# Grouped-query attention: fewer chunks of x transposed on TensorE, eight heads per chunk, and one weight load issued by ScalarE

## Chip, cores, metric

One core of one Trainium2 chip. The metric is device time in microseconds (us) of one execution.

Words used below. PE is TensorE, PEld its weight loads, DVE VectorE, ACT ScalarE, SP SyncE; SPq is the stretch in which SP is occupied with issuing a DMA. A **chunk** is one of the eight 128-column slices of x that the projection sums over. **Rows of chunk n** are the 128 rows of the weight matrix that belong to it. In the profile lines w_sb holds the weights of the first eight heads and wq_sb those of heads 8 and up. A DMA has **landed** when the last of its 16 semaphore increments has arrived; I read each increment as the share of one of the core's 16 DMA engines, though the trace does not name the engine.

## The reference

Two independent problems A and B, joined along the last axis:

```python
q = (x @ wq).reshape(B, Sq, Hq, Dh)      # B=16, Sq=32, D=1024, Hq=32, Dh=128
scores = einsum(q, k) * Dh**-0.5         # k, v shared by groups of 8 heads, Sk=512
o = einsum(softmax(scores), v)
out = o.reshape(B, Sq, Hq*Dh) @ wo       # bf16 throughout
```

## The kernel before

Everything after the first 20 us is a tightly interleaved stream of matmuls. The change touches only the start: the projection of problem A's first eight heads (the **first-head block**), for which x must be transposed (contraction on partitions) and the first weights fetched. SP issues nearly all loads, in program order:

```python
# NF = 6, HC = 4, DC = 8, TT = 4, REP = 8 ; load_w0(d0, d1, h0, h1): rows of chunks d0..d1, heads h0..h1
nc.scalar.preload_act_table_set("natural_log_exp_and_others")
load_x(0, 0, TT // 2)          # chunks 0,1 of x, first half of the tokens, plain, 128 KB
load_x(0, TT // 2, TT)         # second half, 128 KB
load_w0(0, 1, 0, NF // 2)      # 96 KB
load_w0(0, 1, NF // 2, NF)     # 96 KB
load_w0(1, 2, 0, NF)           # 192 KB
load_x(2, 0, TT)               # chunks 2,3 of x, plain, 256 KB
load_w0(2, 3, 0, NF)           # 192 KB
load_w0(3, 4, 0, NF)
load_w0(0, HC, NF, REP)        # heads 6,7 of chunks 0..3
load_w0(HC, HC + 1, 0, REP)    # 256 KB
load_x_transposed(HC)          # chunks 4,5 by a transposing load
load_w0(HC + 1, DC - 1, 0, REP)
load_x_transposed(HC + 2)      # chunks 6,7
load_w0(DC - 1, DC, 0, REP)
load_wq(0, 2, 0, 2)            # heads 8.. ; then keys, values, further weights
# ... cut
warm_up(22)                    # 22 matmuls on constants
# ... 8 transposes of chunks 0,1, copied out of PSUM by DVE and ACT; chunk 0 for heads 0..5
first_heads(range(0, NF - 2), (1,))
transpose_x(2, 0, TT, nc.vector.tensor_copy)     # 4 PE transposes and a PSUM copy
transpose_x(3, 0, TT, nc.scalar.copy)
first_heads(range(NF - 2, NF), (1,))
first_heads(range(NF), (2, 3))
first_q += [psum.tile(...) for _ in range(2)]    # cut
first_heads(range(NF, REP), range(HC))           # heads 6,7, chunks 0..3
first_heads(range(REP), range(HC, DC - 1))
# ... chunk 7, copies to qT, then the stream (heads 8 and up, scores, values)
```

## Time and profile before

Median 343.27 us (343.26 to 343.75, 3 runs). The page gives the busy times and the chain of work that ended last:

```profile
span 341.4 us, 5454 instructions
PE 335.0 (98%) x2082; PEld 213.2 (62%) x2121; DVE 265.6 (78%) x336; ACT 185.8 (54%) x209; POOL 46.7 (14%) x206
PE 94%; DVE 1%; issue 1%; DMA 1%; SPq 1%; ACT 0%; POOL 0%; ACTq 0%
```

PE is never free for long, and the chain runs through it. A matmul's busy time is a modelled, pipelined duration, so for exact sums I use start-to-start distances: 0.216 us for a 512-column matmul. The Trainium skill ("Trainium Kernel Development and Optimization", Performance Expectations) warns that matmul busy time says little about the distance to the limit; here it agrees, since a 512-column matmul is shown as 0.38 us long though one starts every 0.216 us. The change can therefore only matter where PE has gaps or by taking work from PE. The timeline of PE in the first 23 us (start, length, engine, line, operation, count; in brackets the idle time before it and who ended it):

```profile
0.93 2.52 PE L516 MATMUL q_ps<-const-bfloat16-1.0 128*128 128x128 bf16 x22 [0.93 <-PEq L694]
3.24 1.06 PE L524 MATMUL xT_ps<-ident,x_sb 128*128 128x128 bf16 x8
4.10 1.60 PE L534 MATMUL q_ps<-xT,w_sb 128*128 128x256 bf16 x9
6.07 1.04 PE L534 MATMUL q_ps<-xT,w_sb 128*128 128x512 bf16 x4 [0.37 <-DMA w_sb<-in_A_wq_dram]
6.94 0.61 PE L524 MATMUL xT_ps<-ident,x_sb 128*128 128x128 bf16 x8
7.61 11.62 PE L534 MATMUL q_ps<-xT,w_sb 128*128 128x512 bf16 x52
19.07 3.62 PE L301 MATMUL q_ps<-xT,wq_sb 128*128 128x512 bf16 x16
```

The block ends at 19.07, where the matmuls on wq_sb begin. It has one wait, 0.37 us for the rows of chunk 1 (landed 6.02). The second set of eight transposes costs 0.45 us in the chain.

### The profile page before, as it was taken

How to read it: one execution, taken by the hardware profiler on the slowest of the kernel's cores; microseconds unless marked ns; L12 is line 12 of the kernel's file. 1: busy time of each engine (PE TensorE's matmuls, PEld its weight loads, DVE VectorE, ACT ScalarE, POOL GpSimd, SP SyncE). 2: the span in 40 equal slices, each digit the busy share in tenths (PEclk: the TensorE clock that was granted, in tenths of full speed). 3: DMA queues.
4: the chain of work that ended last, by engine and by line, in shares of the span. 5: the costliest groups of instructions: out<-in, count | busy, mean ns of one | idle time of the engine just before them, and what ended most of it. 6: DMA issues, size and time to landing. Idle time of an engine off the chain costs nothing.

```text
span 341.4 us, 5454 instructions
## 1 busy us (share of the span) xinstructions
PE 335.0 (98%) x2082; PEld 213.2 (62%) x2121; DVE 265.6 (78%) x336; ACT 185.8 (54%) x209; POOL 46.7 (14%) x206
## 2 busy tenths in 40 slices
PE   8999999999999999999999999999999999999996
PEld 6455666666666666666666666666666666666555
DVE  1046988888988898888888988879888888889540
ACT  3058666666667667666645545555555555555110
POOL 0001110011111111110012221222122101111100
PEclk9999999999999999999999999999999999999999
DMA  6989999999999988999999956999449996340001
GB/s 192 289 166 286 287 219 241 192 198 276 302 282 203 232 231 221 212 302 288 325 274 266 276 135 142 335 256 250 117 109 292 355 206 160 95 113 10 18 18 33
DMA packets 128094, 71.70 MB, mean 210 GB/s; under 512 B 75840, under 2 KB 127296, under 8 KB 128064
## 3 DMA queue, kind: packets, MB, share of 16 engines
q1 hardware_dynamic: 127536, 70.21, 85.3%
q0 software_dynamic: 384, 1.05, 0.8%
q8 instruction: 17, 0.28, 0.3%
q14 instruction: 13, 0.11, 0.1%
q10 hardware_dynamic: 144, 0.07, 0.1%
HBM read 50.86 MB, written 2.10 MB: 155 GB/s over the span
## 4 chain that ended last, share of the span: by engine, by line
PE 94%; DVE 1%; issue 1%; DMA 1%; SPq 1%; ACT 0%; POOL 0%; ACTq 0%
PE f_ps L320 30%; PE q_ps L301 28%; PE ob L425 17%; PE s_ps L357 16%; PE q_ps L534 4%; DMA w_sb<-in_A_wq_dram 1%; DVE parts L376 1%; ACT p_sb L365 0%; SPq L465 0%; SPq L477 0%; DVE r L411 0%; DVE oT L447 0%; PE xT_ps L524 0%; DVE cs L384 0%; ACT o_sb L329 0%
## 5 line engine op out<-in xcount | busy, mean ns | idle before, releaser
L365 ACT ACTIVATE p_sb<-s_ps,shift 128x1024 bf16<-128x1024 f32 x128 | 142.6, 1114 | 97.7 <-PE s_ps L357 86.2
L376 DVE TRANSPOSE_TENSOR_REDUCE parts<-p_sb 128x32 f32<-128x1024 bf16 x128 | 158.7, 1240 | 21.0 <-ACT p_sb L365 19.3
L320 PE MATMUL f_ps<-wo_sb,oT 128*128 128x512 bf16 (+1 forms) x525 | 128.2, 366 | 0.6
L301 PE MATMUL q_ps<-xT,wq_sb 128*128 128x512 bf16 x430 | 113.3, 379 | 0.5
L425 PE MATMUL ob<-p_sb,v_sb 128*128 128x256 bf16 x512 | 76.8, 273 | 0.8
L357 PE MATMUL s_ps<-qT,kT 128*128 128x256 bf16 x512 | 76.8, 273 | 0.0
L320 PEld LDWEIGHTS <-oT 128*128 128x128 bf16 x544 | 53.2, 98 | 35.4
L357 PEld LDWEIGHTS <-kT 128*128 128x128 bf16 x512 | 56.9, 113 | 28.3
L301 PEld LDWEIGHTS <-wq_sb 128*128 128x128 bf16 x448 | 43.7, 98 | 32.4 <-DMA wq_sb<-in_A_wq_dram 0.4
L425 PEld LDWEIGHTS <-v_sb 128*128 128x128 bf16 x512 | 50.0, 98 | 20.1
L447 DVE TENSOR_TENSOR oT<-r,ob 128x512 bf16<-128x512 f32 x64 | 43.9, 686 | 19.9 <-PE ob L425 19.4
L411 DVE STREAM_TRANSPOSE r<-rall 128x512 f32<-128x512 f32 x64 | 44.2, 691 | 1.1
L309 ACT CAST qT<-q_ps 128x512 bf16<-128x512 f32 x56 | 32.6, 583 | 16.6 <-PE q_ps L301 16.6
L394 POOL COPY half<-cs 64x32 f32<-64x32 f32 x32 | 6.5, 204 | 232.0 <-DVE cs L384 232.0
L329 ACT CAST o_sb<-f_ps 128x512 bf16<-128x512 f32 (+1 forms) x17 | 9.5, 559 | 23.6 <-PE f_ps L320 23.6
L534 PE MATMUL q_ps<-xT,w_sb 128*128 128x512 bf16 (+1 forms) x65 | 14.2, 372 | 0.5 <-DMA w_sb<-in_A_wq_dram 0.4
L384 DVE TENSOR_REDUCE cs<-parts 128x32 f32<-128x128 f32 x32 | 12.1, 377 | 1.1
L406 DVE RECIPROCAL rall<-sums 128x32 f32<-128x32 f32 x32 | 10.2, 318 | 3.3 <-POOL sums L403 3.3
L534 PEld LDWEIGHTS <-w_sb 128*128 128x128 bf16 x67 | 6.4, 99 | 7.6 <-DMA w_sb<-in_A_wq_dram 0.9
L560 DVE CAST qT<-q_ps 128x512 bf16<-128x512 f32 x4 | 2.5, 684 | 10.2 <-PE q_ps L534 10.2
L331 POOL DMA_DIRECT2D out_dram<-o_sb x8 | 4.6, 574 | 29.3 <-ACT o_sb L329 29.3
L395 POOL TENSOR_TENSOR half<-half,cs 64x32 f32<-64x32 f32 x32 | 7.8, 242 | 2.6
(25 smaller groups left out, 44.8 us busy)
## 6 DMA issues: line engine op xcount, KB each, us to landing
v_sb<-in_A_v_cache_dram SPq DMA_DIRECT2D x16, 512.0 KB, 6.3
wq_sb<-in_B_wq_dram SPq DMA_DIRECT2D x8, 1024.0 KB, 5.9
wo_sb<-in_A_wo_dram SPq DMA_DIRECT2D x8, 1024.0 KB, 7.6
v_sb<-in_B_v_cache_dram SPq DMA_DIRECT2D x16, 512.0 KB, 4.6
wo_sb<-in_B_wo_dram SPq DMA_DIRECT2D x8, 1024.0 KB, 8.2
wq_sb<-in_A_wq_dram SPq DMA_DIRECT2D x5, 1024.0 KB, 6.6
wq_sb<-in_A_wq_dram SPq DMA_DIRECT2D x2, 512.0 KB, 7.4
kT<-in_A_k_cache_dram SPq DMA_TRANSPOSE x64, 4.4
```

The source lines that it names most:

```text
L301: nc.tensor.matmul(ps[:], lhsT=w[:, dc, (h % 4) * DH:(h % 4 + 1) * DH], rhs=xT[pr][:, dc, :], start=(dc == 0), stop=(dc == DC - 1),)
L309: nc.scalar.copy(out=qT[pr, g][:, :, hl, :], in_=ps[:].rearrange("p (b s) -> p b s", s=SQ),)
L320: nc.tensor.matmul(ps[:, 0:width], lhsT=oT[pr, tt][:, h, :], rhs=wo_tiles[pr, nh, h // REP][:, h % REP, off:off + width], start=(h == 0), ...
L357: nc.tensor.matmul(s_ps[:, c, :], lhsT=kT[:, i % GRP, c, :], rhs=qT[pr, g][:, b, :, :].rearrange("p h s -> p (h s)"), start=True, stop=True,)
L365: nc.scalar.activation(out=p_sb[:], in_=s_ps[:], func=ACTF.Exp, bias=shift[:], scale=SCALE)
L376: nc.vector.tensor_reduce(out=parts[k][:, q, :, :].rearrange("p c h -> p (c h)"), in_=st[i]["p"][:].rearrange("p c (h s) -> p (c h) s", s=SQ),
L384: nc.vector.tensor_reduce(out=cs[:], in_=parts.pop(k)[:].rearrange("p q c h -> p q h c"), axis=AX.X, op=ALU.add,)
L406: nc.vector.reciprocal(out=rall[:, k, :], in_=quad.pop(k)[:])
L411: nc.vector.transpose(out=r[:].rearrange("p n s -> p (n s)"), in_=rall[:, k, o * 2 * REP:(o + 1) * 2 * REP] .unsqueeze(2).to_broadcast([P, ...
L425: nc.tensor.matmul(ob[j][:, q, :], lhsT=v_sb[:, i % GRP, c, :], rhs=st[i]["p"][:, c, :], start=(c == 0), stop=(c == KC - 1),)
L447: nc.vector.tensor_tensor(out=out, in0=rcp.pop(j)[:].rearrange("p (q h) s -> p q h s", h=REP), in1=ob.pop(j)[:].rearrange("p q (h s) -> p ...
L534: nc.tensor.matmul(first_q[h][:, ts], lhsT=w0[dc // HC][:, dc % HC, h * DH:(h + 1) * DH], rhs=xT[0][:, dc, ts], start=(dc == 0 and t0 == 0 ...
```

## The change

Its intent: drop eight PE transposes and their copies by letting a transposing load bring chunks 2 and 3 of x, use each chunk for all eight heads at once with full 2 KB weight rows, and start the first weight rows sooner from ScalarE's otherwise idle queue.

```diff
+            load_w0(0, 1, 0, NF // 2, nc.scalar)
             nc.scalar.preload_act_table_set("natural_log_exp_and_others")
-            load_x(0, 0, TT // 2)
-            load_x(0, TT // 2, TT)
-            load_w0(0, 1, 0, NF // 2)
+            load_x(0, TT // 2)
+            load_x(TT // 2, TT)
             load_w0(0, 1, NF // 2, NF)
             load_w0(1, 2, 0, NF)
-            load_x(2, 0, TT)
-            load_w0(2, 3, 0, NF)
-            load_w0(3, 4, 0, NF)
-            load_w0(0, HC, NF, REP)
+            load_w0(0, 2, NF, REP)
+            load_x_transposed(2)
+            load_w0(2, 3, 0, REP)
+            load_w0(3, 4, 0, REP)
+            load_x_transposed(HC)
             load_w0(HC, HC + 1, 0, REP)
-            load_x_transposed(HC)
 ... cut (x_sb is smaller, load_w0 takes the issuing engine)
-            first_heads(range(0, NF - 2), (1,))
-            transpose_x(2, 0, TT, nc.vector.tensor_copy)
-            transpose_x(3, 0, TT, nc.scalar.copy)
-            first_heads(range(NF - 2, NF), (1,))
-            first_heads(range(NF), (2, 3))
+            first_heads(range(NF), (1,))
             first_q += [...]
-            first_heads(range(NF, REP), range(HC))
-            first_heads(range(REP), range(HC, DC - 1))
+            first_heads(range(NF, REP), (0, 1))
+            first_heads(range(REP), range(2, DC - 1))
```

More of the change, by code (lines that the diff above doesn't have):

```diff
@@ L456, in fast_path @@
             HC = DC // 2
-            x_sb = blk_tile([P, TT, HC * P], "x_sb")
+            x_sb = blk_tile([P, TT, 2 * P], "x_sb")
             xT[0] = blk_tile([P, DC, NTOK], "xT")
@@ L462, in fast_path, with load_x @@
             wq_v = A_wq.rearrange("(c p) n -> p c n", p=P)
-            def load_x(d0, t0, t1):
-                nc.sync.dma_start(
-                    out=x_sb[:, t0:t1, d0 * P:(d0 + 2) * P],
-                    in_=x_v[:, t0:t1, d0 * P:(d0 + 2) * P],
-                )
+            def load_x(t0, t1):
+                nc.sync.dma_start(out=x_sb[:, t0:t1, :], in_=x_v[:, t0:t1, 0:2 * P])
             def load_x_transposed(d0):
@@ L474, in load_x_transposed, with load_w0 @@
                 )
-            def load_w0(d0, d1, h0, h1):
-                nc.sync.dma_start(
+            def load_w0(d0, d1, h0, h1, eng=nc.sync):
+                eng.dma_start(
                     out=w0[d0 // HC][:, d0 % HC:(d1 - 1) % HC + 1, h0 * DH:h1 * DH],
```

## The prediction

> **What bounds it now.** TensorE: the page gives PE 335.0 us busy of a 341.4 us span at full granted clock, and the chain that ended last is 94% PE. The change touches only the first 20 us; I read that stretch from the timeline and the DMA issues with their landings.
>
> - PE warms up from 0.93 us, transposes x from 3.24, runs the first real matmul at 4.10; the first-head block ends near 19.1. Its 64 matmuls of 512 columns at 0.216 us are 13.8 us, so about 1.2 us of it is not matmul: the second eight transposes (0.45 us in the chain), a wait of 0.37 us for the weight rows of chunk 1 (landed 6.02), small edges.
> - After that PE is fed just in time by the SyncE queue. The tightest place is not in the block: the weights of head 12 (wq_sb issued 21.52, landed 27.27) are awaited at 27.32, with a 0.04 us bubble: slack zero. Next comes the first v_sb (landed 31.64, used 32.5).
>
> **What the change does.**
> - Removes 8 PE transposes (0.45 us) and two PSUM copies; the wait for chunk 1 should shrink, because its rows go out one issue (about 0.5 us) sooner. PE's possible gain: 0.6 to 0.9 us.
> - Replaces a plain 256 KB load of x by a transposing one. In before, one of 256 KB holds SyncE 1.33 or 2.54 us (plain: 0.43 to 0.58) and lands 5.5 to 6.0 us after issue; the first one's 256 B packets fill about 2 us of DMA (8.5 to 10.6), where 256 KB of plain 2 KB rows take about 0.8. The Trainium skill, "Advanced Engine Details and Errata", X-Bar Transpose (TRN2), says transposing DMAs "are as fast as regular DMAs"; this trace disagrees. Extra DMA time, estimated: 0.6 to 1 us. Merging weight rows to 2 KB pieces gives back 0.1 to 0.2.
> - ScalarE issues 96 KB. The skill, "DMA: Bandwidth & Descriptors", Issuing engines are not separate DMA queues, says this saves only sequencer time: here one slot of 0.5 us. Its table load (1.28 us) moves back but ends before ScalarE's first copy at 3.9. The 96 KB share the engines with x, whose second half may land 0.1 to 0.3 us later.
>
> **On the critical path.** Chunk 2 is wanted near 7.6 us. Its transposed x should land near 7.5, the weights behind it near 8.2 to 8.6: a new wait of 0.3 to 1 us, which eats the saved transposes. Chunk 4 may wait 0.2. So the block should end at 18.6 to 19.4. Then the zero-slack weights of head 12: the queue ahead of them drains 0.2 to 0.7 us later, so they land at 27.4 to 28.0. An earlier PE only waits longer there. After it PE is saturated and the shift stays to the end.
>
> **Predicted:** 343.5 us, 342.7 to 344.6. Faster by over 2%: 0.01; within 2%: 0.98; slower: 0.01. The most there is to gain (about 1 us) is 0.3%.
>
> **What would show it.** Right: 64 first-head matmuls after 8 transposes; a PE wait of 0.3 to 1 us at 7.5 to 8.6 us for transposed x or its weights; a longer wait for wq_sb before head 12; later work shifted by a constant. Wrong: no wait at chunk 2, or head 12's weights landing before 27.2.
>
> **What would make it wrong.** If early transposing loads run faster with an emptier queue, the DMA shift is zero or negative and up to 0.8 us is gained; if packets of two queues hamper each other, the first matmul slips and 1 to 2 us are lost.

## The result

344.12 us median (343.18 to 344.27, 6 runs) against 343.37 (343.26 to 343.82, 6 runs): ratio 1.0015, interval 1.0002 to 1.0028. A ratio is the mean time of one kernel's fast runs over that of the other's of the same rounds, so it is not quite the ratio of the medians. By the 2% rule this is "same"; the interval says slightly slower. One of the six runs, 343.18, was as fast as before; its trace does not exist, so why stays open.

The page after, same parts:

```profile
span 342.3 us, 5436 instructions
PE 334.5 (98%) x2074; PEld 212.6 (62%) x2113; DVE 265.1 (77%) x335; ACT 185.1 (54%) x208; POOL 46.6 (14%) x206
PE 95%; DMA 2%; SPq 1%; issue 1%; ACT 0%; ACTq 0%
```

PE has 0.5 us less work, the span is 0.9 us longer. The timeline of PE after:

```profile
0.93 2.52 PE L513 MATMUL q_ps<-const-bfloat16-1.0 128*128 128x128 bf16 x22 [0.93 <-PEq L687]
3.83 0.74 PE L521 MATMUL xT_ps<-ident,x_sb 128*128 128x128 bf16 x8 [0.38 <-DMA x_sb<-in_A_x_dram]
4.61 3.66 PE L531 MATMUL q_ps<-xT,w_sb 128*128 128x256 bf16 x19
9.61 10.53 PE L531 MATMUL q_ps<-xT,w_sb 128*128 128x512 bf16 x47 [1.35 <-DMA w_sb<-in_A_wq_dram]
19.98 3.19 PE L301 MATMUL q_ps<-xT,wq_sb 128*128 128x512 bf16 x13
```

The second set of transposes is gone; the first set waits 0.38 us for x; and a new wait of 1.35 us stands before the first matmul of chunk 2, ended by the weights, not by the transposed x. The block ends 0.91 us later. The sum, start to start: first real matmul later, +0.51 (4.10 to 4.61); the one wait for weights 1.51 instead of 0.53, +0.98; transposes, -0.45; matmuls still at half clock at the very start, -0.13 (explained at the end). That is +0.91. After the block nothing more happens: the first score matmul is 0.91 later (22.52, 23.43), the last matmul of all 0.87 (338.07, 338.94).

The chain of waits in order of time names the weight load. Before, and after:

```profile
2.73 3.29 DMA w_sb<-in_A_wq_dram
6.02 0.05 issue
6.07 1.04 PE q_ps L534 x4
```

```profile
3.21 1.33 SPq L468
4.54 0.05 issue
4.59 4.97 DMA w_sb<-in_A_wq_dram
9.56 0.05 issue
9.61 0.39 PE q_ps L531
```

After, SP is held 1.33 us by issuing the transposing load (SPq L468), then issues the rows of chunk 2 at 4.59, and these take 4.97 us to land. Before, they were issued at 3.68 and took 3.67 us. So they went out 0.91 us later and took 1.30 us longer.

A rule that these lines suggest, and that the experiments use, as long as PE's clock has risen: **the block ends at the latest of (a landing, plus the PE work that stands behind it).** Before: 6.07 plus 13.00 us of gapless PE work is 19.07. After: 9.61 plus 48 matmuls of 0.216 (10.37) is 19.98.

### The profile page after: what moved, and what is told of

Its sections match the earlier page's. It is cut to its first block, busy times and chain, and to the rows that moved or that the text cites. A ratio compares the mean times of both kernels' runs of the same rounds, so it can differ in the third digit from the quotient of the medians.

```text
span 342.3 us, 5436 instructions
## 1 busy us (share of the span) xinstructions
PE 334.5 (98%) x2074; PEld 212.6 (62%) x2113; DVE 265.1 (77%) x335; ACT 185.1 (54%) x208; POOL 46.6 (14%) x206
## 4 chain that ended last, share of the span: by engine, by line
PE 95%; DMA 2%; SPq 1%; issue 1%; ACT 0%; ACTq 0%
PE f_ps L320 31%; PE q_ps L301 28%; PE ob L425 17%; PE s_ps L357 16%; PE q_ps L531 3%; DMA w_sb<-in_A_wq_dram 1%; DMA out_dram<-o_sb 0%; SPq L468 0%; SPq L474 0%; ACT o_sb L329 0%; SPq L465 0%; ACTq L329 0%; ACT p_sb L365 0%; ACTq L365 0%
## 5 line engine op out<-in xcount | busy, mean ns | idle before, releaser
L447 DVE TENSOR_TENSOR oT<-r,ob 128x512 bf16<-128x512 f32 x64 | 43.9, 686 | 19.9 <-PE ob L425 19.4
L309 ACT CAST qT<-q_ps 128x512 bf16<-128x512 f32 x56 | 32.6, 582 | 16.6 <-PE q_ps L301 16.6
L553 ACT CAST qT<-q_ps 128x512 bf16<-128x512 f32 x4 | 2.1, 600 | 13.6 <-PE q_ps L531 13.6
```

What stands on the lines that cost most here:

```text
L309: nc.scalar.copy(out=qT[pr, g][:, :, hl, :], in_=ps[:].rearrange("p (b s) -> p b s", s=SQ),)
L447: nc.vector.tensor_tensor(out=out, in0=rcp.pop(j)[:].rearrange("p (q h) s -> p q h s", h=REP), in1=ob.pop(j)[:].rearrange("p q (h s) -> p ...
```

## The experiments

Theories at the outset. **Q** (queue order): the rows of chunk 2 land late because they stand behind the transposing load. **B/L** (bytes): what counts is how much must be in before PE can go on; by the first matmul of chunk 2 that is 1280 KB after, 1088 KB before. **A**: the ScalarE issue delays x and that is the loss. **S**: a chance late landing. Labels beginning with a_ edit the changed kernel, with b_ the kernel before. Twelve kernels were run, each with 5 rounds. The block end is that of the one profiled run, whose time lies up to 0.5 us from its kernel's median. The overview:

| label | median (before beside it) | ratio, interval | block end in trace | what set it (landing) |
|---|---|---|---|---|
| a_again | 343.87 (343.32) | 1.0014, 1.0001 to 1.0027 | 20.00 | rows of chunk 2, 9.58 |
| a_rows2_ahead | 343.89 (343.32) | 1.0017, 1.0003 to 1.0031 | 19.96 | rows of chunks 5,6, 14.72 |
| a_plain_x23 | 344.32 (343.32) | 1.0029, 1.0017 to 1.0041 | 19.93 | x chunks 2,3, 7.76 |
| a_first_on_sync | 344.37 (343.32) | 1.0029, 1.0016 to 1.0042 | 19.65 | rows of chunk 2, 9.23 |
| b_first_on_scalar | 344.06 (343.36) | 1.0019, 1.0005 to 1.0032 | 19.79 | rows of chunk 1, 6.74 |
| b_xT23 | 344.02 (343.36) | 1.0017, 1.0003 to 1.0031 | 19.88 | rows of chunk 3, 9.90 |
| b_heads8 | 345.39 (343.36) | 1.0047, 1.0033 to 1.0061 | 21.28 | rows of chunk 2, 10.00 |
| b_rows1_on_scalar | 345.88 (343.36) | 1.0067, 1.0053 to 1.0081 | 21.26 | x at 4.41, then the PE clock |
| b_rows1_scalar_late | 343.43 (343.54) | 0.9993, 0.9979 to 1.0006 | 19.23 | rows of chunk 0, heads 3 to 5, 5.54 |
| b_half1_scalar_late | 343.86 (343.54) | 1.0010, 0.9996 to 1.0023 | 19.62 | the PE clock |
| b_first_in_front | 343.35 (343.54) | 1.0004, 0.9991 to 1.0018 | 19.10 | rows of chunk 1, 6.06 |
| b_rows1_not_awaited | 343.35 (343.33) | 1.0003, 0.9989 to 1.0016 | 19.46 | the PE clock |

### a_again: the changed kernel once more

No edit.

> The changed kernel once more, for a second trace. Theory Q (queue order: the weight rows of chunk 2 stand behind the transposing load of x chunks 2 and 3 and land late because of it): the PE wait before the first chunk 2 matmul comes again at 1.0 to 1.5 us, the rows land at 9.3 to 9.8, time 344.0 to 344.3. Theory S (chance: a few of the 16 increments of that landing happened to be late, 8.65 to 9.56 against 8.06 to 8.12 for the rest): the wait differs by over 0.4 us from the first trace, and single times scatter between 343.2 and 344.3.

Measured: the rows landed at 9.58, the wait was 1.18 us in the timeline of PE, the times 343.82 to 344.26. The wait is in the expected range and within 0.2 us of the first trace, so it is no accident of one run: S falls as the explanation of the whole. The shape of the landing repeats too. In the first trace 11 of its 16 increments were in by 8.12 us and the last at 9.56; in the second 14 by 8.89 and the last two at 9.51 and 9.58. The load waits for its last one or two increments.

### a_rows2_ahead: the rows of chunk 2 ahead of the transposing load

```diff
-            load_x_transposed(2)
             load_w0(2, 3, 0, REP)
+            load_x_transposed(2)
```

> The changed kernel with the weight rows of chunk 2 issued ahead of the transposing load of x chunks 2 and 3. Theory Q: the rows land before 7.5 us, the transposed x at 7.7 to 8.3; the wait at chunk 2 falls from 1.35 to at most 0.5 us and the time to 343.2 to 343.5. Theory B (bandwidth: what counts is only how much data must be in, whatever its order): the later of the two still lands near 9.5 and the time stays at 344.0 to 344.3.

Measured: Q's landings came out: rows at 7.47 (expected before 7.5), transposed x at 8.49 (0.2 us after the expected 7.7 to 8.3), and no wait at chunk 2. Q's time did not: 343.89, the same as the changed kernel. PE's timeline shows where the wait went:

```profile
4.71 7.56 PE L531 MATMUL q_ps<-xT,w_sb 128*128 128x256 bf16 x35
12.78 7.34 PE L531 MATMUL q_ps<-xT,w_sb 128*128 128x512 bf16 x32 [0.51 <-DMA w_sb<-in_A_wq_dram]
19.96 0.81 PE L301 MATMUL q_ps<-xT,wq_sb 128*128 128x512 bf16 x3
```

The rows of chunk 4, again a load next to a transposing one, came late (13 of 16 increments by 11.23, the last at 12.74), and the rows of chunks 5 and 6 at 14.72 instead of 13.49; that landing plus its 24 matmuls is the end. So Q explains which load was late, not how much time was lost. Taking one limit away uncovered the next, 0.02 us below.

### a_plain_x23: the transposing load of chunks 2 and 3 undone

```diff
-            load_x_transposed(2)
+            load_x(2, 0, TT)
 ... and the old order of PE work, with its eight transposes
```

> The changed kernel with x chunks 2 and 3 loaded plainly again and transposed on TensorE, in the old order of TensorE work; the merged weight rows and the issue by ScalarE stay. If the transposing load is the cost (theories Q and B): no wait over 0.4 us at chunk 2, time 343.2 to 343.5, as before the change or a little under. If the issue by ScalarE is the cost (theory A: its 96 KB delay x and with it everything): time stays at 343.9 to 344.3.

Measured: 344.32, no better than the changed kernel and rather worse. There is no wait over 0.4 us at chunk 2; instead the first matmul is at 4.69, x chunks 2 and 3 land at 7.76 (6.84 before the change), and 7.80 plus 0.46 us of transposes plus 54 matmuls is the end. The time fits A, but a_first_on_sync refutes A. Note that the order of PE work is the old one here, so the early rows of heads 6 and 7 only take queue space: the run tests the transposing load, not a clean combination of the other two parts.

### a_first_on_sync: the ScalarE issue undone

```diff
-            load_w0(0, 1, 0, NF // 2, nc.scalar)
 ...
             load_x(TT // 2, TT)
+            load_w0(0, 1, 0, NF // 2)
```

> The changed kernel with the first weight rows issued by SyncE, third in its queue, as before the change. Both theories: first transposes back at 3.24 us (from 3.83), first real matmul at 4.1. Theory Q: the wait at chunk 2 then only grows by what was won plus the later issue, to 1.8 to 2.4 us, and the time is 344.1 to 344.7, no better. Theory A: about 0.5 us is won, time 343.5 to 343.8.

Measured: first transposes at 3.24, first real matmul at 4.09, as both theories said. Time 344.37, no better, as Q said. The size of the wait was missed: 0.56 us, not 1.8 to 2.4. In this trace PE ran at half clock until 6.1 us and so reached chunk 2 late by itself; and the rows landed at 9.23, a little sooner than before the edit. A alone is out: 0.5 us won at the start of the block is swallowed by the next landing. The trace is of the fastest of the five runs (343.93); why the other four took 344.25 to 344.58 is not on record.

### The three parts one at a time

**b_first_on_scalar**: only the issue by ScalarE.

```diff
+            load_w0(0, 1, 0, NF // 2, nc.scalar)
             nc.scalar.preload_act_table_set("natural_log_exp_and_others")
 ...
-            load_w0(0, 1, 0, NF // 2)
```

> The kernel before with one part of the change alone: the first weight rows issued by ScalarE. Theory A (the first x shares the DMA engines with these 96 KB): first transposes at 3.8 to 3.9 us instead of 3.24, first real matmul at 4.6 to 4.7; the rows of chunk 1 then land before they are wanted, so its wait of 0.37 us goes; first-head block ends at 19.2 to 19.4 and the time is 343.4 to 343.7. If the early slip is swallowed by a later landing all the same: 343.2 to 343.4.

Measured: 344.06; transposes at 3.90, first matmul at 4.72, as theory A said for the slip. The rows of chunk 1 did not come in time: 6.74 (6.02 before), still awaited (0.22 us), and 6.79 plus the same 13.00 us is 19.79. The loss is larger than either side expected.

**b_xT23**: only the transposing load of chunks 2 and 3.

```diff
-            load_x(2, 0, TT)
+            load_x_transposed(2)
 ...
-            transpose_x(2, 0, TT, nc.vector.tensor_copy)
-            transpose_x(3, 0, TT, nc.scalar.copy)
```

> The kernel before with another part alone: x chunks 2 and 3 by a transposing load, six heads per chunk as before. Theory Q: first matmul stays at 4.10; the rows of chunk 2, queued behind the transposing load, land at 8.8 to 9.5 and PE waits 1.2 to 2 us for them, although 0.45 us of transposes are gone; time 344.2 to 344.8. If the transposing load is harmless by itself: no wait over 0.5 us, time 342.8 to 343.2.

Measured: 344.02, a little under the expected range. First matmul 4.13. The rows of chunk 2 landed at 8.04, sooner than expected but later than with the plain load (7.34), and those of chunk 3 at 9.90 (8.14): two waits, 0.76 and 0.39 us in the timeline, for 0.45 us of transposes saved. The mechanism is Q's; the size was split over two loads. Two things differ ahead of these rows, and this run does not separate them. The transposing load held SP for 1.33 us where the plain one took 0.43, so the two loads behind it went out 0.91 and 0.98 us later. And in each half microsecond from 5.0 to 6.5 us, with the transposing load's packets under way, the DMA moved 184 to 218 GB/s at a busy share of 0.95 or more; before it was 240 to 375 GB/s. The transposed x itself, issued at the same 3.20, landed only 0.29 us after the plain one (7.13, 6.84).

**b_heads8**: only the eight heads per chunk, with x chunks 2 and 3 plain.

```diff
+            load_w0(0, 2, NF, REP)
             load_x(2, 0, TT)
-            load_w0(2, 3, 0, NF)
-            load_w0(3, 4, 0, NF)
-            load_w0(0, HC, NF, REP)
+            load_w0(2, 3, 0, REP)
+            load_w0(3, 4, 0, REP)
 ... and heads 6,7 used for chunks 0..2 right after heads 0..5
```

> The kernel before with the third part alone: weight rows of all eight heads per chunk, loaded and used in that order; x chunks 2 and 3 still plain. Theory L (loads ahead: 128 KB of rows of heads 6 and 7 now go ahead of x chunks 2 and 3, and 64 KB more ahead of what chunk 2 needs): x chunks 2 and 3 land at 7.2 to 7.6 instead of 6.84, rows of chunk 2 at 8.0 to 8.4 instead of 7.34, waits of 0.4 to 0.8 us in addition, time 343.4 to 343.9. If only the transposing load or the ScalarE issue cost anything: 343.1 to 343.4.

Measured: 345.39 (344.62 to 345.6), far worse than expected. x chunks 2 and 3 landed at 7.35, as L said; the rows of chunk 2 at 10.00, not 8.0 to 8.4:

```profile
7.39 0.62 PE L524 MATMUL xT_ps<-ident,x_sb 128*128 128x128 bf16 x8 [0.40 <-DMA x_sb<-in_A_x_dram]
7.85 0.59 PE L534 MATMUL q_ps<-xT,w_sb 128*128 128x512 bf16 x2
10.04 10.75 PE L534 MATMUL q_ps<-xT,w_sb 128*128 128x512 bf16 x49 [1.60 <-DMA w_sb<-in_A_wq_dram]
```

The direction of L holds. Its size does not: the first increment came at 7.24, ten of 16 by 7.72, the last at 10.00. No transposing load stands ahead of these rows, so late increments need none. In a_plain_x23, with 1280 KB wanted by chunk 2 too, the same rows landed at 8.41. What makes single increments late I could not settle. Part of the cost is not the loads' at all: heads 6 and 7 of chunks 0 and 1, whose rows landed at 6.27, are used only after heads 0 to 5 of chunk 2 in this edit. So 52 matmuls stand behind the landing, not 48 as in the changed kernel: 0.86 us more.

The three parts alone cost 0.19%, 0.17% and 0.47%; together 0.15%. They don't add, because the block ends at the latest of its limits: each part pushes a different landing past the old limit, and together they overlap. That b_heads8 alone costs more than the whole change comes from the 0.86 us of PE order and a landing at 10.00 instead of 9.56.

### Does the second queue help? b_rows1_on_scalar, b_rows1_scalar_late, b_half1_scalar_late

The only visible wait before the change is for the rows of chunk 1. Three candidates issue them from ScalarE: at once; held back by a one-column ACT copy into the same tile; and held back, only heads 3 to 5.

```diff
 b_rows1_on_scalar
             nc.scalar.preload_act_table_set("natural_log_exp_and_others")
+            load_w0(1, 2, 0, NF, nc.scalar)
 ...
-            load_w0(1, 2, 0, NF)
 b_rows1_scalar_late, in addition
             nc.scalar.preload_act_table_set("natural_log_exp_and_others")
+            nc.scalar.copy(out=w0[0][:, 1, 0:1], in_=warm[:, 0:1])
             load_w0(1, 2, 0, NF, nc.scalar)
 b_half1_scalar_late: the copy and the ScalarE load cover heads NF // 2 to NF; SP keeps
             load_w0(1, 2, 0, NF // 2)
```

> A candidate: the kernel before with the rows of chunk 1, its only visible wait, issued by ScalarE after its table load (near 2.1 us), when the data of the first x are nearly through. If early transfers are limited by SyncE issuing one every 0.5 us: first matmul stays at 4.10, the rows land at 5.2 to 5.6 instead of 6.02, the wait of 0.37 us goes, time 342.8 to 343.0. If they are limited by the engines or the memory: they land near 6 again, or x chunks 2 and 3 land later and the wait moves there, time 343.2 to 343.5.

Measured: 345.88. My premise was wrong at once: ACT issued the load at 0.85 us and not after its table load, so 192 KB met the first x. That made it an unplanned double dose of the suspected cost: x landed at 4.41 and 4.60 (with 96 KB from ScalarE, in b_first_on_scalar, 3.85 and 4.07; with none, 3.09 and 3.46). PE idled 1.01 us, and the clock rose only near 8.5 us.

> The candidate again, now held back: a one-column copy by ScalarE into the same tile, after its table load, must end before ScalarE issues the rows of chunk 1, so the issue falls at 2.3 to 2.5 us and not at 0.85. If only the collision with the first x made the last candidate slow: x lands at 3.1 and 3.5 us and the first matmul is at 4.10 as before; the rows of chunk 1 land at 5.4 to 5.8 (before: 6.02), block end 18.6 to 18.9, time 342.9 to 343.2, unless the weights of head 12 then become the limit at about 27.3. If a second queue costs something whenever it is used: the first weight rows or the rows of chunk 1 land no earlier than before, time 343.3 to 343.8.

Measured: held back to 2.34 us, x is unharmed (3.23 and 3.59), first matmul 4.11. The rows of chunk 1 landed at 5.81, at the edge of the expectation, but the rows of chunk 0 for heads 3 to 5, in SP's queue beside them, slipped from 4.83 to 5.54, and PE waits 0.58 us for those. The block ended at 19.23, not at 18.6 to 18.9. 343.43 against 343.54, interval across 1: no proven gain.

> The same held-back issue, but only for the second half of the rows of chunk 1 (heads 3 to 5, 96 KB); the first half stays third-last in SyncE's early queue. If smaller pieces land sooner: first half at 5.1 to 5.5, second at 5.4 to 5.9, time 342.9 to 343.2. If a second queue costs whenever it is used: 343.3 to 343.8.

Measured: the halves landed at 5.42 and 5.22 and no wait for DMA is left in the block. Yet 343.86: PE ran at half clock until about 6.5 us in this trace. The data came as hoped; the time did not. The clock is not all of it: of the 0.9 us by which the profiled run's span is longer than before (342.3, 341.4), 0.4 us lie after the start of the last matmul (338.57, 338.07), which I did not follow up.

### b_first_in_front: the same order of bytes in one queue

```diff
+            load_w0(0, 1, 0, NF // 2)
             load_x(0, 0, TT // 2)
             load_x(0, TT // 2, TT)
-            load_w0(0, 1, 0, NF // 2)
```

> The kernel before with the first weight rows (96 KB) at the front of SyncE's own queue instead of third: the same order of bytes as with the issue by ScalarE, but one queue. If a second queue really saves a slot of 0.5 us: x lands 0.3 to 0.5 us later than with the issue by ScalarE (3.8 and 4.0), so at 4.1 to 4.5, and the time is 343.8 to 344.3. If it saves nothing, because two queues together move no more in that time: x lands at 3.5 to 3.7 and 3.9 to 4.1, first matmul at 4.5 to 4.7, time 343.4 to 344.0.

Measured: x at 3.41 and 4.05, first matmul at 4.33, time 343.35, nearest to the "saves nothing" side, though the first half of x and the first matmul came a little sooner than it said. Though SP issued x 0.41 to 0.45 us later than beside ScalarE's load, the first half landed 0.44 sooner than in b_first_on_scalar (3.85) and the second at the same time (4.07). The windows of PE with clock, DMA share and GB/s, between 2.0 and 3.0 us: the kernel before, b_first_in_front, b_first_on_scalar, and the changed kernel:

```profile
2.00:2.50 0.50, 0.50 (x8) 1.00 0.83 247
2.50:3.00 0.50, 0.50 (x7) 1.00 0.90 256
```

```profile
2.00:2.50 0.50, 0.50 (x8) 1.00 0.76 231
2.50:3.00 0.50, 0.50 (x7) 1.00 0.75 217
```

```profile
2.00:2.50 0.50, 0.50 (x8) 1.00 0.39 118
2.50:3.00 0.50, 0.50 (x7) 1.00 0.86 257
```

```profile
2.00:2.50 0.50, 0.50 (x8) 1.00 0.45 135
2.50:3.00 0.50, 0.50 (x7) 1.00 0.94 294
```

With two engines issuing at the very start, the first half microsecond moves half as much (118 and 135 GB/s against 231 and 247), with the DMA engines busy only 39% and 45% of the time. The data were not waiting for bandwidth then; issuing together was itself slower. The table load that the edit pushes back is not the reason: in b_rows1_on_scalar it ran at 0.82 as before, and the rate was 154 GB/s. Which unit is shared, these traces do not show.

### b_rows1_not_awaited: what the one wait is worth

```diff
-    lhsT=w0[dc // HC][:, dc % HC, h * DH:(h + 1) * DH],
+    lhsT=w0[dc // HC][:, 0 if dc == 1 and h < NF else dc % HC, h * DH:(h + 1) * DH],
```

> Wrong result on purpose: the kernel before, but the six matmuls of chunk 1 read the weight rows of chunk 0, which are there, so the one wait of 0.37 us is gone and nothing else is changed. It measures how much that wait is worth. If the weights of head 12 have no slack, as predicted: the block ends 0.3 to 0.5 us earlier, then PE waits longer for those weights (they land near 27.3) and the time is the same within 0.1 us, 343.3 to 343.5. If they can come earlier, or another limit does not follow: 342.8 to 343.1. If the clock of TensorE happens to rise late (after 5.4 us) in the profiled run, the block ends late all the same and the missing wait is used up by half-speed matmuls.

Measured: 343.35 against 343.33. (The comparison with the reference still passed within its tolerance although these rows were wrong, so it can't serve as a check here.) The wait is gone, and in the profiled run the block still ended late, at 19.46, for the third reason I had listed. The line's matmuls of this kernel in two windows of 0.8 us (busy and count for PE, then for PEld, granted clock, DMA share, GB/s):

```profile
5.40:6.20 0.80, 0.80 (x3) 0.28 (x2) 1.00 1.05 348
8.20:9.00 0.80, 0.80 (x5) 0.38 (x4) 1.00 1.09 358
```

The same 512-column matmuls, PE busy throughout, the clock column at 1.00 both times; but three touch the first window and five the second (start to start 0.427 and 0.216 us). Until 6.3 us PE ran at half speed. The clock column cannot show it: the first clock record in the packed trace begins where the distances halve (here at 6.28 us, in the kernel before at 4.36), and time without a record reads as 1.00. Head 12's weights landed at 25.93 and nobody waited for them. So a missing wait at 6 us is worth nothing in such a run. In the unprofiled runs the fastest, 343.26, is also the fastest of the kernel before beside it (343.25); what holds those I cannot say without their traces. The record has one hint, the mean granted clock of every run. The three traces with 0.998 or 0.999 are those in which the clock rose last (6.28, 6.59, 8.56 us). Of the 38 runs of the kernel before beside the experiments, the eight with such a mean took 343.50 to 343.86, the other thirty 343.06 to 343.77, on average 0.3 us less. A late clock may thus be part of the scatter; it is not shown run by run.

## Why the prediction was right or wrong

The time (343.5 expected, 344.12 measured, range 342.7 to 344.6) lay inside the range, slower as expected, within 2%. That the number came out is in part luck. The shift that the prediction carried to the end was a later landing of head 12's weights; they landed earlier. The shift that was measured comes from the end of the block, which lay outside its predicted range. One of the prediction's own signs of being wrong came true ("head 12's weights landing before 27.2"), and so did half of what it said would make it wrong: the first matmul slipped (0.51 us), as if two queues hampered each other, though the kernel lost 0.75 us and not 1 to 2. The mechanism, point by point:

- **"Chunk 2 ... a new wait of 0.3 to 1 us, which eats the saved transposes": right in kind, mis-sized.** The transposed x landed at 7.47 (predicted near 7.5). The term that failed is "the weights behind it near 8.2 to 8.6": they landed at 9.56 and 9.58 in two traces. I had counted bytes at an even rate; a landing is the time of the last of 16 increments, and the last came 1.4 us after the eleventh. The wait was 1.35 us.
- **"The 96 KB share the engines with x, whose second half may land 0.1 to 0.3 us later": mis-sized.** The first half landed 0.69 us later (3.09 to 3.78), the second 0.52 (3.46 to 3.98), and the first matmul slipped 0.51. I took the sharing for one of bandwidth. b_first_in_front shows that the same bytes in one queue, x issued later, let the first half in earlier, and b_rows1_on_scalar that the delay grows with the ScalarE load.
- **"The wait for chunk 1 should shrink": right in the record, for the wrong reason.** Its rows landed at 5.88 instead of 6.02, 0.14 us sooner and not 0.5; the wait went mostly because PE came later.
- **"Extra DMA time, estimated: 0.6 to 1 us": not measured by itself.** The 2 us that I took for one transposing load held packets of other loads and a stall. Where the queue was full, 256 KB took 0.99 us transposed and 0.71 plain (after, landing to landing: 13.49, 14.48, 15.19). I had left out that the loads behind also go out later (0.91 us in b_xT23).
- **A later wait at chunk 4 and at head 12: wrong.** The weights of head 12 landed at 26.09, 1.18 us earlier than before, and PE's weight load asked for them at 27.98: no wait, where I had foretold 27.4 to 28.0 and a longer one. The wq_sb load was issued at 20.39 instead of 21.52; the four transposing loads of keys ahead of it held SP for 2.44, 1.26, 1.26 and 1.76 us instead of 3.84, 2.22, 1.27 and 1.26. I extrapolated a queue shift over more than ten loads; it did not survive the varying times for which SP was held in between. Why that fell out so is not settled.
- **"The block should end at 18.6 to 19.4": wrong**, 19.98, as the sum of the first two points. **"Later work shifted by a constant": right**, +0.91 at 20 us, +0.87 at 338 us.

What the experiments put in place of my single-cause account: no part of the change gains alone, each undoing only uncovers the next landing, and the end of the block is the latest of several limits (in the traces of the four a_ kernels it lies between 19.65 and 20.00). Shown: the ScalarE issue at the start delays x; the transposing load delays the rows behind it (7.34 to 8.04 and 8.14 to 9.90 in b_xT23); loading all eight heads first delays what chunk 2 needs. Only argued: that single slow engines do the rest. No version tried beats the kernel before; the four whose interval lies across 1 tie with it.

## What to carry to other kernels

At the start of a kernel, list every load with its landing and the work behind it; the end is the largest sum, and removing work that is not behind the largest sum gains nothing. Be wary of letting a second engine issue bulk loads while the first, most urgent ones are being set up; hold it back with a real dependency if it must be used, and check when it issued. Count how long a load holds the engine that issues it, and not only its bytes: all its later loads go out later. Before believing half a microsecond near the start, look at matmul start-to-start distances to see when the clock rose in that very run.

## What the Trainium skill lacked or had wrong

- "DMA: Bandwidth & Descriptors", Issuing engines are not separate DMA queues, says that issuing from several engines at once only saves the issuing time. Here it cost time: from 2.0 to 2.5 us the DMA moved 118 and 135 GB/s with two engines issuing, 231 and 247 with one, and the first 128 KB of x landed at 3.85 and 3.78 us instead of 3.41 and 3.09 (b_first_on_scalar and after, against b_first_in_front and before).
- "TensorE: Matmul & The Clock Gate", Part 1: The HAM clock gate, explains the half-speed start by a free-running activity window and puts its scatter at 500 ns either way (a note in the same section allows more: 6, 11 or 14 slow matmuls in one kernel). The kind agrees; the 500 ns do not. In 14 traces, all with PE starting at 0.93 us, start-to-start distances halved between about 4.0 and 6.5 us in 13 and at 8.5 us in the one whose PE idled for 1.0 us at 3.45. Before: near 4.4; after: near 4.1, hence the -0.13 us in the sum above.
- "Advanced Engine Details and Errata", X-Bar Transpose (TRN2), calls transposing DMAs as fast as regular ones and expects 350 to 400 GB/s. Where the queue was full, 256 KB took 0.99 us transposed (265 GB/s) and 0.71 us plain in the after trace. It says nothing of the issue: each transposing load of x held SP for 1.2 to 2.9 us in the before, after and b_xT23 traces, against 0.43 to 0.58 for a plain load of x or of w_sb, and in b_xT23 the next two loads landed 0.7 and 1.8 us later.
- No page that I found says this: packets of a transposing load can stay open together and all end together, here soon after the last, late increment of a load ahead (9.54 before, 9.56 after). Whether the one holds the other is not shown. Before, 19 such 256 B packets, started between 9.20 and 9.66, all ended between 10.07 and 10.11; after, 19, started between 8.71 and 9.58, between 10.09 and 10.12, the longest open for 1.39 us. The 16 increments of the plain load just ahead followed within 10.13 to 10.27. In the windows of PE after, the share of 1.91 (open packets count as busy) and then only 66 GB/s show this stall:

```profile
8.00:9.00 1.00, 0.26 (x2) 1.00 1.91 252
9.00:10.00 1.00, 0.39 (x1) 1.00 0.47 66
```
